# Value products of a 16-head attention, two key blocks at a time behind every second block's scores

## Chip, cores and metric

The kernel runs on 1 core of one Trainium2 chip. The metric is the device time of one execution in microseconds (us). Three timed runs of the kernel before gave 745.59, 741.81 and 741.84 us, median 741.84 us.

## What is computed

Three stages follow each other in one launch: a bucketed softmax attention (2 batches of 8 heads, 768 rows, 64 columns a head), a two-layer network with a squared ReLU over 1536 tokens, and a mixture of 8 experts with one expert a token. The change touches the attention alone:

```python
mask = q_bucket[:, :, :, None] == k_bucket[:, :, None, :]      # sign bits of q @ proj and k @ proj
scores = scale * np.matmul(q, k.transpose(0, 1, 3, 2))
scores = np.where(mask, scores, -1000000000.0)
scores = scores - np.max(scores, axis=-1, keepdims=True)
attn = np.exp(scores)
attn = attn / (np.sum(attn, axis=-1, keepdims=True) + 1e-09)
return np.matmul(attn, v).astype(np.float32)
```

## The kernel before, in words

The 16 heads (2 batches times 8) are numbered h = 0 to 15, two heads make a pair p, and each head has NB = 6 key blocks j of 128 keys. `Attn.program` (L482) writes out the order of the whole attention by hand: `at(g, pri, fn)` puts a step into group g with a priority, the list is sorted by 10 g + pri, and every engine gets its instructions in that order. Group g = 6 h + j holds block j of head h. For the heads from 4 on a group holds, in this order:

- `st(h, j)` (L396, priority 1): the scores of one key block against all 768 queries, four matmuls of 384 columns (tile `Sst`). ScalarE takes the exponential into the tile `e` (L405), and, except for block 5, makes a 16-bit copy `eh` (L411); GpSimd makes the rest `el = e - eh` (L412).
- `maxp` of the head two further on (L350, priority 2, 12 groups ahead): two matmuls (tile `Smaxp`) and a VectorE maximum `mx` (L359).
- `avs(h, j, t)` (L418), the value products of the block two groups back (`LAG = 2`), in two halves t = 0 and 1 at priorities 5 and 7 (`a0`, `a1`): 18 matmuls for a block with `eh` and `el`, and for block 5 (`WHOLE`) 6 matmuls on the 32-bit `e` (tile `VW`) with 6 on the small tiles `NM` and `VS`. They add up in a tile `av` of their own (pool `psA`).

Once a head or once a pair of heads other steps stand in a group, at priority 8 behind both halves or at 0 ahead of the scores: `mrow` (L383, tile `Smrow`, once a head in the group of a block 2), `xt` (L455, tile `Sxt`, ahead of a block 4), the two `trans` (L185, tiles `Strans` of q and of k) and `bits` (L235, tile `Sbits`).

What ties these steps together is the pool `psS` (L1363, opened in `fused_kernel`, 3 buffers): `Sst`, `Smaxp`, `Smrow`, `Sxt`, `Strans` and `Sbits` all come from it, each of two PSUM banks. Three tiles are there, so a step on TensorE that needs a new one waits until the reader of an older one is done: ScalarE's exponential for `Sst`, VectorE's maximum for `Smaxp`.

```python
psA = pool("psA", 1, **P)
psS = pool("psS", 3, cs, **P)
```

Behind the attention, from about group 81 on, the decoding of the next stage's weights (`w_next`, L659, lines L705 to L735) is mixed into the same queues of ScalarE, VectorE and GpSimd; the 16 groups of heads 14 and 15 have no `maxp`.

Of the kernel before, what the change touches and what calls it, by code (L numbers as in the profile page):

```python
# [25 lines left out]
LAG = 2  # L26
# [3 lines left out]
XN = [[f"x{g}{i}" for i in "hl"] for g in range(3)]  # L30
AT = dict(vx=-2, tq=-20, tk=-19, bits=-17, mo=-6, mr=2, xt=21, mx=-12, vs=4,
          tpri=8, bpri=0, vpri=8, mopri=6, mrpri=8, xpri=8, fpri=3, mxpri=2, a0=5, a1=7)


def f(ap):
# [7 lines left out]
class Attn:  # L43
# [438 lines left out]
    def program(self):  # L482

        ev = []

        def at(g, pri, fn, *a):
            ev.append((10 * g + pri, len(ev), fn, a))

        NP = self.NP
        n = iter(range(-100, -9))  # L490
        pre = lambda fn, *a: at(next(n), 0, fn, *a)
        gp = self.nc.gpsimd
        pre(self.load, 0)
        pre(self.setup2)
        pre(self.zero_set, gp, 0)
        pre(self.setup2b)
        for p in range(1, 4):
            pre(self.zero_set, gp, p)
        for p in range(1, 4):
            pre(self.load_v, p)  # L500
        pre(self.trans, 0, "q")
        pre(self.asm, 0, "q", (0,))
        pre(self.trans, 0, "k")
        pre(self.asm, 0, "k", (0,))
        pre(self.bits0, "q")
        pre(self.bits0, "k")
        pre(self.setup3)
        for x in "qk":
            pre(self.asm, 0, x, (1,))
        pre(self.load_v, 0, self.nc.sync)  # L510
        for x in "qk":
            pre(self.asm, 1, x, (0,))
        pre(self.load, 1)
        for x in "qk":
            pre(self.asm, 1, x, (1,))
        pre(self.maxp, 0, 0)
        pre(self.maxp, 0, 1)
        pre(self.bits1, 0)
        pre(self.maxp, 0, 2)
        pre(self.vabs, 0)  # L520
        for j in range(3, NB):
            pre(self.maxp, 0, j)
        pre(self.vscan, 0, 1)
        pre(self.mops, 0)
        pre(self.bits2, 0)
        pre(self.asm_aux, 1)
        pre(self.mrow, 0)
        pre(self.vscale0, 0)
        pre(self.vscale1)
        at(0, 2, self.vscale2, 0)  # L530
        at(0, 2, self.vxs, 0)
        pre(self.vmask)
        at(1, 2, self.vx, 0)
        at(1, 6, self.vsums, 0, 1)
        for hh in range(2):
            at(1 + hh, 4, self.vxl, 0, hh)
        for i, p in enumerate(range(1, 4)):
            at(1 + 2 * i, 9, self.vabs, p)
            at(3 + 2 * i, 9, self.vred, p)
        at(6, 9, self.vscale0, 1)  # L540
        at(8, 0, self.vscale1)
        at(9, 4, self.vscale2, 1)
        at(9, 9, self.vscan, 1, 4)
        at(10, 9, self.vsums, 1, 4)
        for i, p in enumerate(range(4, NP)):
            at(6 + i, 9, self.load_v, p)
            at(13 + 2 * i, 9, self.vabs, p)
            at(14 + 2 * i, 9, self.vred, p)
        at(20, 9, self.vscale0, 2)
        at(22, 0, self.vscale1)  # L550
        at(23, 4, self.vscale2, 2)
        at(23, 9, self.vscan, 4, 8)
        at(24, 9, self.vsums, 4, 8)
        for j in range(NB):
            at((1, 1, 2, 2, 3, 3)[j], 3, self.maxp, 1, j)
            at((6, 7, 7, 8, 8, 9)[j], 3, self.maxp, 2, j)
            at((10, 11, 11, 12, 13, 13)[j], 2, self.maxp, 3, j)
        for p in range(NP):
            g = 12 * p
            if p:  # L560
                if p > 1:
                    at(g - 32 + 3 * (p == 3), 0, self.load, p)
                s = ((0, 1, 4), (7, 8, 9))[p - 1] if p < 3 else (g + AT["tq"], g + AT["tk"], g + AT["bits"])
                for n, x in enumerate("qk"):
                    at(s[n], AT["tpri"], self.trans, p, x)
                    if p == 1:
                        at(2, 6, self.asm, 2, x, (0,))
                        at(2, 7, self.asm, 2, x, (1,))
                        at(4, 9, self.asm, 3, x, (0,))
                        at(5, 4, self.asm, 3, x, (1,))  # L570
                    else:
                        at(s[1] + 1, 6, self.asm, 2 * p, x)
                        at(g - 12, 0, self.asm, 2 * p + 1, x)
                at(s[2], AT["bpri"], self.bits, p)
                at(s[2], 9, self.asm_aux, 2 * p)
                at(5 if p == 1 else g - 12, 0, self.asm_aux, 2 * p + 1)
                at(g - (4 if p > 1 else 3), 9, self.vxs, p)
                at(g - 2, AT["vpri"], self.vx, p)
                for hh in range(2):
                    at(g - 1 + 2 * hh, AT["vpri"], self.vxl, p, hh)  # L580
            at(g + AT["vs"], 9, self.vsel, p)
            if p < NP - 1:
                at(g + AT["xt"], AT["xpri"], self.xt, p)
        for h in range(2 * NP):
            for j in range(NB):
                g = 6 * h + j
                i = g % 12
                at(g, 1, self.st, h, j)
                if h > 3:
                    at(g + AT["mx"], AT["mxpri"], self.maxp, h, j)  # L590
                at(g + LAG, AT["a0"], self.avs, h, j, 0)
                at(g + LAG, AT["a1"], self.avs, h, j, 1)
            g = (-29, 4, 9, 14)[h] if h < 4 else 6 * h + AT["mo"]
            if h:
                at(g, 4 if h < 4 else AT["mopri"], self.mops, h)
                at((0, 5, 10, 16)[h] if h < 4 else g + AT["mr"], (0, 0, 7, 8)[h] if h < 4 else AT["mrpri"], self.mrow, h)
            at(6 * h + 6 + LAG, AT["fpri"], self.fin, h)
        ev.sort(key=lambda e: e[:2])
        return [(e[0] // 10, (lambda e=e: e[2](*e[3]))) for e in ev]
# [876 lines left out]
```

## Time and profile before

| | |
|---|---|
| median of 3 runs | 741.84 us |
| the profiled execution, its own time | 740.73 us |
| span of that execution's profile | 738.9 us |
| TensorE busy, matmuls | 691.1 us (94%) |
| TensorE busy, weight loads | 606.7 us (82%) |
| VectorE / ScalarE / GpSimd busy | 429.1 / 364.6 / 248.0 us |
| mean granted TensorE clock | 0.975 of full speed |

The time is the whole device execution; the span is what the profile of one execution covers, 1.8 us less. PE is TensorE's matmuls, PEld its weight loads, DVE is VectorE, ACT ScalarE, POOL GpSimd. Matmuls overlap in the records, so their busy time reads higher than what is really filled; the weight loads stand behind each other.

### The profile page before, as it was taken

The numbers are of one execution on the slowest core, as the hardware profiler recorded it, in microseconds if no ns is written. First come the engines' busy times: TensorE is split into PE (matmuls) and PEld (weight loads), VectorE is DVE, ScalarE is ACT, GpSimd is POOL, SyncE is SP. The second block draws the span as 40 slices with busy tenths as digits, with TensorE's granted clock in tenths as the row PEclk, the third lists the DMA queues.
The fourth block names the chain that finished last, engine by engine and source line by source line (L and its number), as shares of the span: only waits on it lengthen the run. The fifth ranks groups of instructions, "written<-read, shape, count | busy, mean of one in ns | idle before, by whom it ended". The sixth has DMA issues, their size and how long they took to land.

```text
span 738.9 us, 12831 instructions
## 1 busy us (share of the span) xinstructions
PE 691.1 (94%) x5037; PEld 606.7 (82%) x5037; DVE 429.1 (58%) x781; ACT 364.6 (49%) x562; POOL 248.0 (34%) x251
## 2 busy tenths in 40 slices
PE   6688899999999689999999999999999999999993
PEld 5487789899898568788888888888789889999992
DVE  5456767667667977888783322235663674545311
ACT  2565787877878755555542232222350344344412
POOL 8295877776878860000000000200020104040102
PEclk9799999999999889999999999999999999999997
DMA  6979435655470221443420010001440545445101
GB/s 147 218 168 226 98 73 113 141 110 114 109 186 2 87 86 59 151 134 114 142 59 0 1 44 14 1 16 43 130 144 1 175 157 191 129 136 151 58 17 44
DMA packets 53509, 73.64 MB, mean 100 GB/s; under 512 B 30456, under 2 KB 30968, under 8 KB 53440
## 3 DMA queue, kind: packets, MB, share of 16 engines
q1 hardware_dynamic: 50320, 63.49, 32.6%
q0 software_dynamic: 2960, 9.24, 4.0%
q8 instruction: 41, 0.67, 0.4%
q14 instruction: 28, 0.23, 0.1%
q10 hardware_dynamic: 160, 0.00, 0.0%
HBM read 46.37 MB, written 6.49 MB: 72 GB/s over the span
## 4 chain that ended last, share of the span: by engine, by line
PE 68%; ACT 8%; issue 7%; DVE 7%; POOL 4%; DMA 3%; SPq 1%; POOLq 0%; ACTq 0%; DVEq 0%
PE Y L863 17%; PE H L820 16%; PE H L1161 8%; PE Y L1181 7%; PE Sst L403 5%; PE av L424 5%; ACT e L405 4%; PE Smaxp L357 2%; PE Sbits L240 2%; POOL el L412 2%; ACT eh L411 1%; PE ml L891 1%; DVE v L716 1%; DMA nq<-in_q_dram 1%; PE Strans L192 1%
## 5 line engine op out<-in xcount | busy, mean ns | idle before, releaser
L412 POOL TENSOR_TENSOR el<-e,eh 128x768 f16<-128x768 f32 x80 | 133.3, 1673 | 64.5 <-ACT eh L411 52.6
L863 PE MATMUL Y<-gh,W 128*128 128x512 f32 x384 | 131.8, 396 | 0.7 <-DVE sv L873 0.7
L359 DVE TENSOR_REDUCE mx<-Smaxp 128x1 f32<-128x768 f32 x96 | 90.3, 953 | 37.9 <-PE Smaxp L357 37.6
L405 ACT ACTIVATE e<-Sst 128x768 f32<-128x768 f32 x96 | 77.0, 803 | 44.6 <-PE Sst L403 42.4
L403 PE MATMUL Sst<-Q,K 128*128 128x384 f32 x384 | 93.5, 366 | 2.1 <-ACT e L405 1.9
L863 PEld LDWEIGHTS Y<-gh,W 128*128 128x128 f32 x384 | 72.1, 188 | 16.8 <-DVE sv L873 1.1
L1181 PE MATMUL Y<-hh,W 128*128 128x408 f32 x256 | 81.5, 359 | 0.0
L827 DVE SCALAR_TENSOR_TENSOR r<-r,sb 128x512 f32<-128x512 f32 x46 | 35.9, 780 | 70.3 <-ACT r L826 70.3
L863 PE MATMUL Y<-gl,W 128*128 128x512 f32 x192 | 75.3, 392 | 0.0
L403 PEld LDWEIGHTS Sst<-Q,K 128*128 128x128 f32 x384 | 65.3, 195 | 5.7 <-ACT e L405 2.8
L411 ACT ACTIVATE eh<-e 128x768 f16<-128x768 f32 x80 | 67.5, 844 | 2.5
L826 ACT ACTIVATE r<-H 128x512 f32<-128x512 f32 x44 | 26.3, 598 | 82.0 <-PE H L820 81.9
L801 POOL IOTA ev<- 128x96 f32 x1 | 0.3, 298 | 192.7 <-PE H L820 192.7
L357 PE MATMUL Smaxp<-K,Q 96*128 96x384 f32 x192 | 50.6, 353 | 10.6 <-DMA Q<-aux 3.5
L1134 POOL DMA_INDIRECT xg<-yd,ix x16 | 17.8, 1110 | 123.2 <-DVE nf L1120 62.8
L834 ACT ACTIVATE gh<-r,sb 128x512 fp32r<-128x512 f32 x46 | 33.1, 721 | 52.7 <-PE Y L863 51.0
L835 DVE SCALAR_TENSOR_TENSOR gl<-r,sb,gh 128x512 fp32r<-128x512 f32 x46 | 34.4, 749 | 37.4 <-ACT gh L834 37.4
L424 PE MATMUL av<-VX,eh 128*128 128x65 f16 x960 | 52.1, 196 | 4.1 <-ACT eh L411 4.1
L424 PEld LDWEIGHTS <-eh 128*128 128x128 f16 x960 | 39.8, 99 | 16.7 <-issue 11.5
L1068 DVE TENSOR_TENSOR W<-st,W 128x1024 fp32r<-128x1024 f32 x32 | 38.8, 1224 | 18.4 <-ACT W L1067 18.4
L1181 PEld LDWEIGHTS Y<-hh,W 128*128 128x128 f32 x256 | 48.0, 188 | 0.0
L357 PEld LDWEIGHTS Smaxp<-K,Q 96*128 96x128 f32 x192 | 35.6, 197 | 14.7 <-issue 4.0
(321 smaller groups left out, 1475.1 us busy)
## 6 DMA issues: line engine op xcount, KB each, us to landing
st<-in_moe_w_dram SPq DMA_DIRECT2D x32, 512.0 KB
sw<-in_moe_w_in_dram SPq DMA_DIRECT2D x16, 512.0 KB
sw<-in_moe_w_out_dram SPq DMA_DIRECT2D x16, 512.0 KB
Q<-qh SPq DMA_DIRECT2D x32, 192.0 KB
K<-kh SPq DMA_DIRECT2D x32, 192.0 KB
nq<-in_q_dram SPq DMA_DIRECT2D x16, 192.0 KB
nk<-in_k_dram SPq DMA_DIRECT2D x16, 192.0 KB
Q<-ql SPq DMA_DIRECT2D x16, 192.0 KB
```

The source lines that it names most:

```text
L357: nc.tensor.matmul(out=ps[:, a, 0:HALF], lhsT=self.Q1[i][0:96, j * 128:j * 128 + 128], rhs=self.K1[i][0:96, a * HALF:a * HALF + HALF])
L359: nc.vector.tensor_reduce(out=self.mx[h][:, j:j + 1], in_=ps[:, :, 0:HALF], axis=AX.XY, op=ALU.max)
L403: nc.tensor.matmul(out=ps[:, a, 0:HALF], lhsT=K[:, c], rhs=Q[:, a * HALF:a * HALF + HALF], start=(n == 0), stop=(n == 1))
L405: nc.scalar.activation(out=h2(e), in_=ps[:, :, 0:HALF], func=ACTF.Exp, scale=0.125)
L411: nc.scalar.activation(out=eh, in_=e, func=ACTF.Copy)
L412: nc.gpsimd.tensor_tensor(out=el, in0=e, in1=eh, op=ALU.subtract)
L424: mm = lambda q, n, e, v, start=False, stop=False: nc.tensor.matmul(out=av[:, q, 0:n], lhsT=e, rhs=v, start=start, stop=stop, skip_group_c ...
L820: nc.tensor.matmul(out=ps, lhsT=w[:, k, fs], rhs=x[:, k], start=(n == 0), stop=(n == 11))
L863: nc.tensor.matmul(out=self.yp[d], lhsT=w[:, i, ds], rhs=x, start=(fc in (0, FA) and n == 0), stop=(fc in (FA - 1, 15) and n == 2))
L1068: nc.vector.tensor_tensor(out=lo[:, o], in0=d["st"], in1=f(hi[:, o]), op=ALU.subtract)
L1161: nc.tensor.matmul(out=ps, lhsT=w, rhs=xx[:, kd, 0:C], start=(n == 0), stop=(n == 11))
L1181: nc.tensor.matmul(out=self.yp[d][:, 0:C], lhsT=w, rhs=xx, start=(fc == 0 and n == 0), stop=(fc == 7 and n == 2))
```

## The change

The value products of the even blocks (j = 0, 2, 4) of heads 4 to 13 move one group later. They then stand in the group of the odd block with that block's own value products: first half of the even block, first half of the odd block, second halves likewise. In the group of an even block no value product is left. This makes 30 pairs of blocks, in groups (26, 27) to (84, 85). Nothing is added or removed: the instructions of ScalarE, VectorE, GpSimd and the DMA queue are the same in the same order, and only TensorE's differ in their order.

```diff
+AV2 = (4, 14)
...
-                at(g + LAG, AT["a0"], self.avs, h, j, 0)
-                at(g + LAG, AT["a1"], self.avs, h, j, 1)
+
+                ga = g + LAG + (j % 2 == 0 and AV2[0] <= h < AV2[1])
+                at(ga, AT["a0"], self.avs, h, j, 0)
+                at(ga, AT["a1"], self.avs, h, j, 1)
```

Two places show it on TensorE. The numbers in the names tell tiles apart; a wait named Activation is one for ScalarE, DVE for VectorE, Pool for GpSimd.

The first place is head 8, blocks 2 and 3, with `mrow` between them. Before ("..." leaves out rows of the same step):

```order
L403 MATMUL Sst_2524<-Q1_0_114,K1_0_115 128x384 [waits DVE_49]
...
L357 MATMUL Smaxp_2535<-K1_2_123,Q1_2_122 128x384 [waits Activation_49]
...
L424 LDWEIGHTS eh_2464
L424 MATMUL av0_2543<-VX0_132,eh_2464 128x65
...
L389 MATMUL Smrow_2562<-identb_59,MP1_131 128x128 [waits DVE_49]
L403 MATMUL Sst_2569<-Q1_0_114,K1_0_115 128x384 [waits Activation_49]
```

In the changed kernel:

```order
L407 MATMUL Sst_2524<-Q1_0_114,K1_0_115 128x384 [waits DVE_49]
...
L361 MATMUL Smaxp_2535<-K1_2_123,Q1_2_122 128x384 [waits Activation_49]
...
L393 MATMUL Smrow_2543<-identb_59,MP1_131 128x128 [waits DVE_49]
L407 MATMUL Sst_2550<-Q1_0_114,K1_0_115 128x384 [waits Activation_49]
...
L361 MATMUL Smaxp_2561<-K1_2_123,Q1_2_122 128x384 [waits DVE_49]
...
L428 LDWEIGHTS eh_2464
```

The value products on `eh_2464` stood between the maximum's matmuls and `mrow`; now they come behind the second scores and their maximum. The second scores take the tile that the first scores had, three tiles back, and wait for ScalarE in both orders.

The second place is head 8, blocks 0 and 1, with no step between them; the second block's group also holds the value products of a block 5. Before:

```order
L403 MATMUL Sst_2457<-Q1_0_114,K1_0_115 128x384 [waits DMAHW6_49,DMAHW5_49,DVE_49]
...
L357 MATMUL Smaxp_2469<-K1_2_123,Q1_2_122 128x384 [waits DMAHW3_49,DMAHW4_49,DMAHW0_49,Activation_49]
...
L424 LDWEIGHTS eh_2392
...
L403 MATMUL Sst_2496<-Q1_0_114,K1_0_115 128x384 [waits DVE_49]
...
L357 MATMUL Smaxp_2507<-K1_2_123,Q1_2_122 128x384 [waits Activation_49]
...
L424 MATMUL av1_2313<-VW1_135,e_2424 128x65 x3
```

In the changed kernel, from the second scores on:

```order
L407 MATMUL Sst_2478<-Q1_0_114,K1_0_115 128x384 [waits DVE_49]
...
L361 MATMUL Smaxp_2489<-K1_2_123,Q1_2_122 128x384 [waits Activation_49]
L361 MATMUL Smaxp_2489<-K1_2_123,Q1_2_122 128x384
L428 LDWEIGHTS eh_2392
L428 MATMUL av1_2337<-VX1_133,eh_2392 128x65
```

The value products on `eh_2392` have moved from ahead of the second scores to behind the second maximum. That maximum takes the tile of the first scores, three tiles back, and waits for ScalarE in both orders.

The third place is head 7, blocks 0 and 1, with `bits` between them. Before:

```order
L403 MATMUL Sst_2204<-Q1_3_126,K1_3_127 128x384 [waits DMAHW7_49,DMAHW0_49,DVE_49]
...
L424 LDWEIGHTS eh_2126
...
L240 MATMUL Sbits_2249<-qh_2159,WQ0_110 128x384 [waits Activation_49]
...
L240 MATMUL Sbits_2249<-kl_2201,WK0_112 128x384 [waits DVE_49]
```

In the changed kernel:

```order
L361 MATMUL Smaxp_2216<-K1_1_119,Q1_1_118 128x384
L244 MATMUL Sbits_2231<-qh_2141,WQ0_110 128x384 [waits Activation_49]
...
L361 MATMUL Smaxp_2257<-K1_1_119,Q1_1_118 128x384 [waits DVE_49]
...
L428 LDWEIGHTS eh_2126
```

Here too the value products that stood ahead of `bits` now stand behind the second maximum; `bits` takes the tile of the first scores of this pair and waits for their exponential.

## Rows read from the trace of the kernel before

**Rows 1.** The page, part 1: busy time, share of the span and instructions.
```profile
PE 691.1 (94%) x5037; PEld 606.7 (82%) x5037; DVE 429.1 (58%) x781; ACT 364.6 (49%) x562; POOL 248.0 (34%) x251
```
**Rows 2.** Busy time by stretch: PE, PEld, DVE, ACT, POOL; PEclk, DMA share, GB/s.
```profile
178.00:206.00 28.00, 27.46 (x326) 25.28 (x326) 19.59 (x32) 21.83 (x32) 21.85 (x20) 1.00 0.45 111
...
231.00:263.00 32.00, 25.07 (x303) 21.56 (x301) 28.75 (x31) 23.68 (x37) 25.86 (x19) 0.89 0.16 51
```
**Rows 3.** Timeline, weight loads, head 10 blocks 0 to 4: start, us, instruction, [idle before].
```profile
186.71 0.65 PEld L403 LDWEIGHTS Sst<-Q,K 128*128 128x128 f32 x4
...
187.87 0.24 PEld L424 LDWEIGHTS <-eh 128*128 128x128 f16 x6 [0.15 <-issue]
...
188.40 0.65 PEld L403 LDWEIGHTS Sst<-Q,K 128*128 128x128 f32 x4
189.03 0.36 PEld L357 LDWEIGHTS Smaxp<-K,Q 96*128 96x128 f32 x2
189.38 0.81 PEld L424 LDWEIGHTS av<-VW,e 128*128 128x128 f32 x6
...
191.02 0.65 PEld L403 LDWEIGHTS Sst<-Q,K 128*128 128x128 f32 x4
...
192.95 0.65 PEld L403 LDWEIGHTS Sst<-Q,K 128*128 128x128 f32 x4
...
194.63 0.65 PEld L403 LDWEIGHTS Sst<-Q,K 128*128 128x128 f32 x4
```
**Rows 4.** Timeline, ScalarE, the exponential of head 10 block 2.
```profile
192.09 0.81 ACT L405 ACTIVATE e<-Sst 128x768 f32<-128x768 f32 x1 [0.93 <-PE Sst L403]
```
**Rows 5.** Timeline, weight loads, from k's transpose to head 11 block 2.
```profile
198.96 0.64 PEld L192 LDWEIGHTS Strans<-ident,nk 128*128 128x128 f32 x6 [0.28 <-ACT e L405]
...
201.49 0.65 PEld L240 LDWEIGHTS Sbits<-qh,WQ 128*128 128x128 f32 x4 [0.17 <-ACT e L405]
...
206.19 0.65 PEld L403 LDWEIGHTS Sst<-Q,K 128*128 128x128 f32 x4
```
**Rows 6.** Timeline, ScalarE, the same stretch.
```profile
199.87 0.81 ACT L196 ACTIVATE kh<-Strans 128x768 fp32r<-128x768 f32 x1 [0.96 <-PE Strans L192]
200.62 0.81 ACT L405 ACTIVATE e<-Sst 128x768 f32<-128x768 f32 x1
```
**Rows 7.** Timeline, weight loads, head 9 blocks 2 to 5.
```profile
178.60 0.65 PEld L403 LDWEIGHTS Sst<-Q,K 128*128 128x128 f32 x4
...
182.22 0.64 PEld L471 LDWEIGHTS Sxt<-ident,xn 128*128 128x128 f32 x6
...
185.03 0.65 PEld L403 LDWEIGHTS Sst<-Q,K 128*128 128x128 f32 x4 [0.45 <-ACT e L405]
```
**Rows 8.** Timeline, matmuls, the same stretch.
```profile
182.25 0.85 PE L471 MATMUL Sxt<-ident,xn 128*128 128x128 f32 x6
...
185.03 0.97 PE L403 MATMUL Sst<-Q,K 128*128 128x384 f32 x4 [0.33 <-ACT e L405]
```
**Rows 9.** Timeline, ScalarE, the same stretch.
```profile
182.67 0.84 ACT L411 ACTIVATE eh<-e 128x768 f16<-128x768 f32 x1
183.42 0.58 ACT L477 ACTIVATE x0h<-Sxt 128x512 fp32r<-128x512 f32 x1
...
184.16 0.81 ACT L405 ACTIVATE e<-Sst 128x768 f32<-128x768 f32 x1
```
**Rows 10.** Waits of the stretch 104 to 231 us: in total, times, longest.
```profile
PEld L424 <- issue: 7.1, 46, 0.2
```
**Rows 11.** Groups of instructions of the same stretch: count, busy, mean ns, idle before.
```profile
L412 POOL TENSOR_TENSOR el<-e,eh 128x768 f16<-128x768 f32 x47 | 77.3, 1652 | 29.8 <-ACT eh L411 22.7 <-PE Smaxp L357 2.2 <-POOL el L412 2.0
```
**Rows 12.** The chain that ended last, 225 to 290 us: start, us, what.
```profile
237.33 0.86 DVE mx L359
238.20 1.69 DVE sw L713
...
262.05 0.51 issue
```

## The prediction

> **What bounds the kernel now.** I read the page's busy shares first, then busy time by stretch, then the timeline of weight loads in one period of the attention, and beside it ScalarE's timeline. TensorE is busy 94% of the span [rows 1], and between 104 and 231 us, where heads 4 to 13 run, its clock is full: in 178 to 206 us the granted clock reads 1.00 (the 2.4 GHz level), weight loads fill 25.28 of 28 us, and VectorE, ScalarE and GpSimd are each busy about 20 to 22 of 28 [rows 2]. So TensorE's order sets the pace there, and weight loads stand behind each other almost without holes. The pattern repeats every 12 blocks (one pair of heads), 27.59 us from 178.60 to 206.19 [rows 5, 7].
>
> A plain block is 1.69 us (186.71 to 188.40): 1.16 to the first value product (scores, maximum, and a hole of 0.15 at the switch from the 32-bit to the 16-bit loads), then 0.53 for the value products. A block whose value products are those of a block 5 takes 2.62 us (188.40 to 191.02), 0.98 up to them and 1.64 for them, with no such hole ahead [rows 3]. The hole is counted 46 times in 104 to 231 us, 7.1 us in all [rows 10].
>
> The number that decides is how long a score tile stays occupied. Scores start at 191.02; their exponential runs from 192.09 for 0.81 us; the next user of that tile starts at 192.95: **1.93 us from start to release** [rows 3, 4]. Before the change the 0.53 us of value products and the hole stand inside these 1.93 us. There TensorE loses next to nothing to the wait: that block with its `mrow` would have ended around 192.8 by itself (191.02 + 1.69 and one short load).
>
> **The change, part by part.** Nothing is added; 27 pairs of blocks lie in groups 26 to 79, three more in the stretch where the weights are decoded. The score pool's tiles go round in the same order in both kernels. In a changed pair, scores, maximum, any step between, scores and maximum follow directly, and both blocks' value products come last. What the pool needs for the fourth tile of that run is the tile of the pair's first scores, so 1.93 us must pass, and only the work left in between hides it. The pairs of one period:
>
> - Blocks 0 and 1 of an even head. Now 186.71 to 191.02, 4.31 us [rows 3]. Changed: the second maximum would start at 1.01 + 0.63 = 1.64 us (scores and maximum of a block without the hole are 189.38 less 188.40, 0.98 to 1.01; scores alone are 189.03 less 188.40) but waits to 1.93; then 0.35 for it, the hole 0.15, 0.53 and 1.64: 4.60. Cost 0.29.
> - Blocks 2 and 3, `mrow` between. Now 191.02 to 194.63, 3.61 us [rows 3]. Changed: the second scores wait to 1.93 with only about 1.2 us of work ahead; then 1.16 and twice 0.53: 4.15. Cost 0.54, one whole block of value products that used to stand under the exponential.
> - Blocks 4 and 5 with q's transpose between, then blocks 0 and 1 of the odd head with k's transpose ahead and `bits` between. Now 194.63 to 206.19, 11.56 us. The first of the two would take 1.93 + 1.16 + 1.06 = 4.15, but k's transpose waits for an exponential anyway and starts at 4.33 (198.96) [rows 5], so nothing is lost there. `bits` starts 2.53 us behind that transpose, set by ScalarE's chain (copy of k at 199.87, exponential at 200.62 for 0.81 [rows 6]), and that chain stays. What stood under it, the hole and 0.53, now comes later. Cost 0.68.
> - Blocks 2 and 3 of the odd head with `mrow`, then `xt`, then blocks 4 and 5. Now 178.60 to 186.71, 8.11 us [rows 3, 7]. Changed: the first pair takes 4.15, so `xt` starts at 4.15 instead of 3.62 (182.22). Its result is there 0.88 later (182.25 + 0.85 against 182.22 [rows 8]), at 5.03, while ScalarE takes it up at 4.82 now (183.42), right behind its 16-bit copy [rows 9]. ScalarE therefore slips by 0.21, and the release of block 4's scores from 6.43 (185.03) to 6.64; then 1.16 and twice 0.53: 8.86. Cost 0.75.
>
> One period costs 0.29 + 0.54 + 0.68 + 0.75 = 2.26 us. Groups 26 to 73 are four periods: 9.0. Groups 74 to 79 have no transposes left: 0.54 for the `mrow` pair, 0.11 for a plain pair (1.93 + 0.35 + 0.15 + 1.06 = 3.49 against 3.38) and 0.29: 0.9. The sum is **10.0 us**.
>
> On the gain side stand only the holes. A period has ten now and keeps eight: the `mrow` pairs go back to 16-bit loads and out again between the blocks, so they keep two. This is already in the sums above; alone it is 2 times 0.15 in each of five periods, 1.5 us.
>
> From group 80 on I charge nothing. From 231 to 263 us VectorE is busy 28.75 of 32 us [rows 2] and carries the chain, from the first decode at 238.20 to 262 [rows 12]; weight loads fill only 21.56 of the 32. The cover is VectorE's decoding; without it the last three pairs would cost up to 1.0 more (0.75 and 0.29). The delay built up before is not absorbed: the first decode stands behind a maximum of the attention (237.33) in VectorE's queue [rows 12], so it starts later with TensorE.
>
> What is late next behind the wait: GpSimd's `el`, 1.65 us each, ten a period with other work, 21.85 of 28 us busy [rows 2, 11]. By estimate a pair's last 16-bit copy ends 4.4 us after the pair's start (1.07 and four ScalarE operations of 0.81 to 0.84) and its `el` at 6.1; the products that need it start at 4.15 + 1.93 + 1.16 + 0.53 = 7.8. I take no loss. The queues of the DMAs are not passed by anything.
>
> The sum stands against the profiled execution's 740.73 us: 750.7. The median of the runs is 741.84, so I predict 741.84 + 10.0 = **751.8 us**.
>
> **A rule against the trace.** Two records at 185.03, the matmul that waited and the weight load of the same scores, start together, behind a hole of 0.45 in the loads [rows 7, 8]: the load did not run ahead of the wait. By the Trainium skill, TensorE: Matmul & The Clock Gate, section "Architectural detail: the array is 16× 32×32, not 1× 128×128", TensorE's queue pulls weight loads ahead of matmuls in flight. By that rule a load would be done within the wait; the row speaks against it for these 32-bit scores.
>
> **Rivals.**
>
> - Weight loads run ahead of the wait. A load of the scores is 0.65 / 4 = 0.16 us [rows 3], and 27 waits would each get one back: 4.3 us, so 747.5. The release of 1.93 was read from start to start and would already hold such a gain; chance 0.06.
> - The release takes longer than 1.93. With ScalarE's other copies in the way it is already 2.17 in one pair of six (scores behind the 0.64 of `xt`'s loads from 182.22, release 185.03 [rows 7]). If the bunched maxima and exponentials make it that in 20 more pairs, or `el` comes late by as much, 20 times 0.24 is 4.8: 756.6. Chance 0.12.
> - Not slower: the delay is eaten in 231 to 263 us. TensorE has about 10 us of unfilled weight-load time there [rows 2], as much as the sum. If the decoding began at a time of its own (its data's arrival), TensorE would come 10 us late into a stretch where it waits anyway, and the time would stay at 741.8. It decides if the first decode does not move with the attention; its place right behind a maximum [rows 12] speaks against it. Chance 0.03.
> - Only the holes count: if ScalarE freed a score tile in 1.6 us, no wait would show and 1.5 us are gained: 740.3. The exponential alone ends 1.88 after the start [rows 3, 4]. For more than 0.5% (3.7 us) every pair would have to lose a hole, 30 times 0.15, 737.3. Chance 0.02, and 0.02 for that second form.
>
> That the change does nothing is excluded: TensorE's rows differ in the three places shown.
>
> **How the numbers follow.** The forecast case has 0.75. Its range goes from the least (weight loads partly ahead, some waits covered: 747) to the last three pairs counted and ScalarE late in places (757); with the neighbouring rivals I take 746.5 to 757.5, which leaves out the not-slower cases and the long tail of late releases. Within 0.5% of 741.84 (3.7 us, about what a measurement here can tell from no change) lie the eaten delay and the lone holes: 0.05. Faster by more: 0.02. Slower by more: 0.93.
>
> **What would show it.** Right: weight loads of the second scores behind `mrow`, and of the second maximum elsewhere, idle 0.3 to 0.7 us before them, released by the exponential; a period of about 29.8 us instead of 27.59; 16-bit holes down from ten to eight a period; the first decode near 248 us instead of 238.20; the rest shifted as a block. Wrong: a period under 28.5, or a first decode that has not moved, or idle time that GpSimd's `el` ends.

## The result, and the profile after

The changed kernel takes 748.26 us (median of 9 runs, 747.74 to 750.41) against 741.81 us of the kernel before in the same series (9 runs). The ratio is 1.0103, with a 95% interval of 1.008 to 1.0127: 7.6 us slower (5.9 to 9.4). The ratio is not that of the two medians, which differ by 6.45 us. Forecast were 751.8 us, 10.0 us slower, in a range of 746.5 to 757.5.

The page, part 1, of the changed kernel (its profiled execution took 750.41 us, span 748.6), to be read beside [rows 1]:

```profile
PE 696.3 (93%) x5037; PEld 610.2 (82%) x5037; DVE 427.2 (57%) x781; ACT 364.3 (49%) x562; POOL 248.0 (33%) x251
```

Counts are the same, and so nearly are the busy times of VectorE, ScalarE and GpSimd. TensorE's records are 5.2 us (matmuls) and 3.5 us (weight loads) longer in sum, but hardly where heads 4 to 13 run. There the time came as idle time. To see it, take the same work in both kernels, from the exponential of head 4 block 2 to that of head 13 block 2, called the **stretch** from here on. Its busy times (columns as in [rows 2]) before and after:

```profile
109.28:231.10 121.82, 119.81 (x1427) 110.06 (x1425) 85.85 (x138) 94.96 (x138) 94.47 (x73) 1.00 0.53 117
```

```profile
111.05:241.60 130.55, 120.93 (x1427) 109.64 (x1425) 83.97 (x138) 95.33 (x138) 94.78 (x73) 1.00 0.49 110
```

The clock is full in both. Weight loads fill 109.64 us instead of 110.06 although the stretch is 8.73 us longer, and the other engines are nearly as busy as before: every engine waits more. The waits of the weight loads show for whom TensorE waits (idle time in total, times, longest). Before, in 104 to 231 us and beside the holes of [rows 10], they are:

```profile
PEld Sst L403 <- ACT e L405: 1.8, 4, 0.5
PEld Strans L192 <- ACT e L405: 1.0, 4, 0.3
PEld Sbits L240 <- ACT e L405: 0.7, 4, 0.2
```

After, the same from 105.8 to 241.5 us, where the same blocks now run:

```profile
PEld Sst L407 <- ACT e L409: 9.8, 13, 0.9
PEld L428 <- issue: 4.4, 28, 0.2
PEld Sbits L244 <- ACT e L409: 3.7, 4, 0.9
PEld L393 <- issue: 1.4, 9, 0.2
PEld Smaxp L361 <- ACT e L409: 1.1, 6, 0.2
```

Waits for ScalarE's exponential went from 3.5 us (12) to 14.6 us (23). The holes at the switch of loads went from 46 (7.1 us) to 37 (28 + 9, 5.8 us). GpSimd's `el` ends none of them. Here is one period, the timeline of weight loads from head 9 block 2 to head 11 block 2 of the changed kernel (columns as in [rows 3]):

```profile
185.45 0.65 PEld L407 LDWEIGHTS Sst<-Q,K 128*128 128x128 f32 x4
...
187.38 0.65 PEld L407 LDWEIGHTS Sst<-Q,K 128*128 128x128 f32 x4 [0.68 <-ACT e L409]
...
189.64 0.64 PEld L475 LDWEIGHTS Sxt<-ident,xn 128*128 128x128 f32 x6
190.25 0.65 PEld L407 LDWEIGHTS Sst<-Q,K 128*128 128x128 f32 x4
...
192.18 0.65 PEld L407 LDWEIGHTS Sst<-Q,K 128*128 128x128 f32 x4 [0.94 <-ACT e L409]
...
194.40 0.65 PEld L407 LDWEIGHTS Sst<-Q,K 128*128 128x128 f32 x4
...
196.29 0.30 PEld L361 LDWEIGHTS Smaxp<-K,Q 96*128 96x128 f32 x2 [0.16 <-ACT e L409]
...
198.86 0.64 PEld L407 LDWEIGHTS Sst<-Q,K 128*128 128x128 f32 x4
...
200.80 0.65 PEld L407 LDWEIGHTS Sst<-Q,K 128*128 128x128 f32 x4 [0.67 <-ACT e L409]
...
203.03 0.65 PEld L407 LDWEIGHTS Sst<-Q,K 128*128 128x128 f32 x4
...
204.90 0.65 PEld L407 LDWEIGHTS Sst<-Q,K 128*128 128x128 f32 x4
...
207.18 0.64 PEld L196 LDWEIGHTS Strans<-ident,nk 128*128 128x128 f32 x6
...
209.71 0.65 PEld L244 LDWEIGHTS Sbits<-qh,WQ 128*128 128x128 f32 x4 [0.93 <-ACT e L409]
...
215.07 0.65 PEld L407 LDWEIGHTS Sst<-Q,K 128*128 128x128 f32 x4
```

The `mrow` pair at 185.45 waits 0.68 us at its second scores, which start 1.93 us behind the first ones. The same wait stands at 200.80, behind `mrow`, 1.94 us after 198.86. From 185.45 to 215.07 a period lasts 29.62 us; it was 27.59.

The stretch serves below as the yardstick for all kernels. It was 121.82 us (109.28 to 231.10) and is 130.55 us (111.05 to 241.60): 8.73 us more. It is used because head 4 block 2, which comes ahead of every changed instruction, stands anywhere from 107.22 to 113.99 us in the executions profiled here; the spans carry that difference, the stretch does not. Behind the stretch the chain of waits of the changed kernel reads:

```profile
248.68 1.68 DVE sw L719
...
272.81 0.51 issue
...
279.57 3.44 PE SH L826 x12
```

Against [rows 12] the first decode is at 248.68 instead of 238.20 and the end of decoding at 272.81 instead of 262.05: 10.48 and 10.76 later, of which 8.73 is the stretch and 1.77 the later start of this execution. The decoding absorbed nothing of the delay.

### The profile page after: what moved, and what is told of

Its sections match the earlier page's. It is cut to its first block, busy times and chain, and to the rows that moved or that the text cites. A ratio compares the mean times of both kernels' runs of the same rounds, so it can differ in the third digit from the quotient of the medians.

```text
span 748.6 us, 12831 instructions
## 1 busy us (share of the span) xinstructions
PE 696.3 (93%) x5037; PEld 610.2 (82%) x5037; DVE 427.2 (57%) x781; ACT 364.3 (49%) x562; POOL 248.0 (33%) x251
## 4 chain that ended last, share of the span: by engine, by line
PE 69%; DVE 7%; issue 6%; ACT 6%; POOL 4%; DMA 4%; SPq 2%; POOLq 0%; ACTq 0%; DVEq 0%
PE Y L869 16%; PE H L826 16%; PE av L428 7%; PE Sst L407 7%; PE H L1167 6%; PE Y L1187 5%; PE Smaxp L361 3%; ACT e L409 3%; PE Sbits L244 2%; PE Strans L196 1%; POOL el L416 1%; PE ml L897 1%; DVE v L722 1%; SPq L187 1%; SPq L210 1%
## 5 line engine op out<-in xcount | busy, mean ns | idle before, releaser
L407 PE MATMUL Sst<-Q,K 128*128 128x384 f32 x384 | 95.2, 372 | 8.7 <-ACT e L409 8.5
L407 PEld LDWEIGHTS Sst<-Q,K 128*128 128x128 f32 x384 | 67.4, 200 | 13.6 <-ACT e L409 11.7
```

Source lines behind the costliest of these rows:

```text
L407: nc.tensor.matmul(out=ps[:, a, 0:HALF], lhsT=K[:, c], rhs=Q[:, a * HALF:a * HALF + HALF], start=(n == 0), stop=(n == 1))
```

## Experiments

Each edit is against the changed kernel. Ratios are to the kernel before, on the same chip.

**1. `mrow` behind the pair.** In the changed kernel only `mrow`'s load of 0.10 us stands between the first maximum and the second scores, which take the first scores' tile. With `mrow` out of the middle the pair is a plain one, in which the second maximum takes that tile.

```diff
-at(... g + AT["mr"], ..., self.mrow, h)
+at(... g + AT["mr"] + (5 <= h <= 14), ..., self.mrow, h)
```

> The changed kernel with mrow of heads 5 to 14 moved one group later, behind both blocks' value products. Yardstick: from the exponential of head 4 block 2 to that of head 13 block 2, 121.8 us before and 130.55 changed; 12 blocks are 27.59 and 29.62. Theory A (a score tile is released 1.9 us after its scores start, and only the work between hides that): the mrow pairs no longer need that tile for the second scores but for the second maximum, later by 0.65; a pair of 4.17 becomes about 3.6. Period about 28.8, stretch about 126.7, time about 4 us under the changed kernel's. Theory B (two blocks' work handed to ScalarE and GpSimd at once comes back late, wherever the other steps stand): period stays near 29.6, stretch near 130.5. Theory C (the wait is due to mrow's own operands): the wait moves with mrow, idle time ahead of its load, period near 29.6.

Stretch 128.17, period 29.11 (expected: 126.7 and 28.8), and 749.08 us (4 runs), ratio 1.0123 (1.0075 to 1.017). The `mrow` pairs became 3.51 and 3.46 us (195.20 to 198.71, 211.06 to 214.52) from 4.17 and 4.19, but part came back later, in new waits for `mrow`'s reader (`NM`). Timeline of weight loads, from head 10 block 3 on:

```profile
197.14 0.30 PEld L361 LDWEIGHTS Smaxp<-K,Q 96*128 96x128 f32 x2 [0.23 <-ACT e L409]
...
198.68 0.10 PEld L393 LDWEIGHTS <-MP 128*128 128x128 bf16 x1
...
200.17 0.64 PEld L196 LDWEIGHTS Strans<-ident,nq 128*128 128x128 f32 x6 [0.45 <-ACT NM L396]
...
216.95 0.30 PEld L361 LDWEIGHTS Smaxp<-K,Q 96*128 96x128 f32 x2 [1.06 <-ACT NM L396]
...
217.64 0.65 PEld L407 LDWEIGHTS Sst<-Q,K 128*128 128x128 f32 x4 [0.39 <-ACT e L409]
```

`mrow` too takes a score tile. It is now read late in ScalarE's queue, behind exponentials, so its tile comes free late. Ahead of `mrow`'s own load (198.68) stands no wait, so its operands were not the cause. The stretch gives back 2.4 of 8.7 us; the timed ratio, of four runs, is not below that of the changed kernel and does not show it.

**2. `bits` behind the value products.** `bits` of the pairs of heads from 4 on moves from between the two scores to behind both blocks' value products.

```diff
-at(s[2], AT["bpri"], self.bits, p)
+at(s[2], 8 if p > 3 else AT["bpri"], self.bits, p)
```

> The changed kernel with bits of pairs 4 to 7 of heads moved from between the two blocks to behind both blocks' value products. Theory A: bits no longer stands under ScalarE's chain (copy of k, then exponential); the 0.93 us of idle time ahead of it goes, of which about 0.3 comes back ahead of the second maximum. 0.6 a period: period about 29.0, stretch about 128.0, time about 2.5 us under the changed kernel's. Theory B: period stays near 29.6.

Stretch 130.46, ratio 1.0123 (1.0071 to 1.0174): the expected 128.0 was missed. The wait did not go; it changed its bearer, as the timeline of weight loads at head 11 blocks 0 and 1 shows:

```profile
207.18 0.65 PEld L407 LDWEIGHTS Sst<-Q,K 128*128 128x128 f32 x4
...
209.11 0.65 PEld L407 LDWEIGHTS Sst<-Q,K 128*128 128x128 f32 x4 [0.93 <-ACT e L409]
...
212.37 0.65 PEld L244 LDWEIGHTS Sbits<-qh,WQ 128*128 128x128 f32 x4
```

The second scores now take the tile that `bits` took, and wait the same 0.93 us, 1.93 us behind the first scores. The wait belongs to the tile, not to the step that takes it. My expectation had overlooked that.

**3. Only the second halves moved.** The first half (0.27 us of value products and a hole) stays between the two scores, half of the cover.

```diff
-at(ga, AT["a0"], self.avs, h, j, 0)
+at(g + LAG, AT["a0"], self.avs, h, j, 0)
```

> The changed kernel with the first half of the even blocks' value products left in their own group, so that only the second half (0.27 of 0.53 us) moves. Theory A: a half left in place covers 0.27 of the release and the hole 0.15; the mrow pair, bits and the xt pair each cost 0.27 instead of 0.54 to 0.75, the plain pairs nothing. 0.8 a period: period about 28.4, stretch about 125.3, time about 3.5 us over the kernel before. Theory B: half the work bunched, half the cost, stretch about 126.2; near, so this run is a dose, not a verdict. If the cost were the switch between 32-bit and 16-bit loads alone, the switches are those of the kernel before and the stretch would be 121.8.

Stretch 124.84, period 28.3, 744.75 us (10 runs), ratio 1.0053 (1.0027 to 1.0079). Timeline of weight loads, the `mrow` pair of head 10 and then `bits`:

```profile
197.76 0.65 PEld L407 LDWEIGHTS Sst<-Q,K 128*128 128x128 f32 x4
...
199.69 0.65 PEld L407 LDWEIGHTS Sst<-Q,K 128*128 128x128 f32 x4 [0.42 <-ACT e L409]
...
208.34 0.64 PEld L244 LDWEIGHTS Sbits<-qh,WQ 128*128 128x128 f32 x4 [0.44 <-ACT e L409]
```

The wait behind `mrow` is 0.42 with half of the value products left in place and 0.68 with none: 0.26 for half a block. The distance from first to second scores is 1.93 in both, and 1.93 in the kernel before, where the whole block fitted inside [rows 3]. At `bits`, whose wait was 0.17 [rows 5], it is 0.44 and 0.93. This is the dose test of the theory, and the stretch came out 0.5 under its number of 125.3. The kernel has the holes of the kernel before (46, 7.2 us in the same blocks) and is still 3.0 us longer in the stretch, so the switches between the loads are not the cost.

**4. The other pairing.** Blocks (1, 2), (3, 4), (5, 0 of the next head) share their value products; as many pairs, as much bunching, but other steps stand between. The step that reads a head's finished value products off `av` (`fin`) moves behind them.

```diff
-ga = g + LAG + (j % 2 == 0 and AV2[0] <= h < AV2[1])
+ga = g + LAG + (j % 2 == 1 and AV2[0] <= h < AV2[1])
...
-at(6 * h + 6 + LAG, AT["fpri"], self.fin, h)
+at(6 * h + 6 + LAG, 9 if AV2[0] <= h < AV2[1] else AT["fpri"], self.fin, h)
```

> The same bunching with the other parity: the value products of the odd blocks of heads 4 to 13 wait for the next even block, and fin of these heads stands behind them. mrow, q's transpose and bits now fall behind the bunched products without being moved; k's transpose and xt stand between the two scores. Theory A: only those two (of six pairs) need the first scores' tile early, and the waits that the kernel before has ahead of k's transpose (0.28) and bits (0.17) go. Summing a period: 4.55 + 4.1 + 4.15 + 2.0 + 4.55 + 4.15 + 3.5 = 27.0 to 27.6; stretch 119 to 122, time between 2.5 us under the kernel before and the same. Theory B: bunched as in the changed kernel, so as slow: period near 29.6, time 6 to 8 us over the kernel before.

Stretch 123.70, periods 27.62, 28.24, 28.22 and 28.32, 744.28 us (12 runs), ratio 1.0044 (1.0018 to 1.007). The stretch is 1.7 us over the first theory's 119 to 122 and far from the second's, which would be about that of the changed kernel. The time, 3.3 us over the kernel before (1.3 to 5.2), lies between the two and does not decide. The longest waits of this kernel's weight loads, 104 to 232.9 us (idle in total, times, longest):

```profile
PEld Smaxp L361 <- ACT e L409: 3.6, 14, 0.3
PEld Strans L196 <- ACT e L409: 3.5, 4, 0.9
PEld L428 <- issue: 3.2, 20, 0.2
PEld Sst L407 <- DVE aux L252: 2.8, 4, 0.7
...
```

Holes fell from 46 to 20, and yet the kernel is slower than before. Plain pairs now wait 0.24 to 0.33 us at the second maximum. The pair with both transposes waits 0.9 us a period, and one wait I had not foreseen is VectorE reading the tile of `bits` (`aux`), which had been covered. Bunching itself is not the cost: the same number of pairs costs 1.9 us of the stretch instead of 8.7 where other steps stand between the scores.

**5. Two pairs a period that looked free**, (2, 3)'s products behind q's transpose and a block 5 with the next block 0.

```diff
-ga = g + LAG + (j % 2 == 0 and AV2[0] <= h < AV2[1])
+ga = g + LAG + (AV2[0] <= h < AV2[1] and (j == 5 if h % 2 else j == 2))
...
-at(6 * h + 6 + LAG, AT["fpri"], self.fin, h)
+at(6 * h + 6 + LAG, 9 if h % 2 and AV2[0] <= h < AV2[1] else AT["fpri"], self.fin, h)
```

> Bunched only where the release theory sees no loss: the value products of a block 5 of an odd head wait for the next head's block 0 (then mrow follows them), and those of block 2 of an even head wait for block 3, in the pair that has q's transpose between. By the traces of the changed kernel and of the one with odd blocks waiting: the first saves about 0.11 a period (4.44 against 4.55), the second 0.18 (4.15 against 4.33, k's transpose no longer waits). Theory A: period about 27.3, stretch about 120.5, time 1 us or so under the kernel before, too little for the time to show alone. Any theory in which bunching costs by itself: two of six pairs bunched, a third of the changed kernel's 8.7, stretch about 124.7.

Stretch 121.94 against 121.82; 740.27 us (12 runs), ratio 1.0011 (0.999 to 1.0032): no difference. The pair at q's transpose takes 4.32 us in both kernels (111.83 to 116.15 before, 115.29 to 119.61 here). The second scores there start 2.04 us behind the first. Timeline of weight loads:

```profile
117.33 0.64 PEld L407 LDWEIGHTS Sst<-Q,K 128*128 128x128 f32 x4 [0.29 <-ACT e L409]
...
217.94 0.64 PEld L407 LDWEIGHTS Sst<-Q,K 128*128 128x128 f32 x4 [0.68 <-DVE mx L363]
```

The nine holes saved (46 to 37, 7.1 to 5.8 us) went into waits for score tiles. The two middle periods of the stretch are 27.44 and 27.41 us, against 27.59 and 27.63 before, so some 0.2 us of the hoped 0.3 a period was there (at the first one the new order moves the mark itself). The wait at 217.94, which stands once and has no counterpart in the kernel before, took it back; its reason was not followed up. Neither number came out for the stretch: the gain of 1.3 us is not there, and the cost of bunching (124.7) is not there either. No version beat the kernel before.

**6. The last three pairs alone, and all but these.** The prediction charged nothing from group 80 on. Four runs ask whether that holds.

```diff
-AV2 = (4, 14)
+AV2 = (13, 14)
```

> The kernel before with only head 13's even blocks moved: the three pairs in groups 80 to 85, where the weights' decoding on VectorE carries the chain. The prediction charged nothing for them, with up to 1.0 us if the decoding were no cover. Cover theory: stretch head 4 block 2 to head 13 block 2 as before (121.8), first decode 7.1 us behind the exponential of head 13 block 2 as before (231.10 to 238.20), time as before. Otherwise: first decode 0.5 to 1.0 later, time up to 1.0 us over the kernel before.

742.9 us (10 runs), ratio 1.0042 (1.0016 to 1.0068), stretch 121.77. To see what is spread and what is cost, the same kernel again, beside one in which no head is changed (`AV2 = (4, 4)`), and one with heads 4 to 12 changed (`AV2 = (4, 13)`):

> No head is changed (the range of heads is empty), so every engine has the order of the kernel before. Theory (only moved value products cost): the time of the kernel before, ratio 0.998 to 1.002, stretch 121.8. Rival (the small excess of the run with the last three pairs comes from the spread between chips and executions at the start of the program, not from the moved products): this kernel too can read up to 1.004 while its stretch stays at 121.8, with head 4 block 2 at 111 us or later instead of 109.

> The same kernel as the run with the last three pairs alone, beside a kernel without any moved product on the same chip. If the moved products behind group 80 cost something (about 0.4%, 3 us), it reads 2 to 4 us more than the kernel without moved products. If the prediction's step (nothing from group 80 on) holds, the two agree within 1.5 us, and the first decode stands 7.1 us behind the exponential of head 13 block 2 again.

> Heads 4 to 12 changed, head 13 (the last three pairs, groups 80 to 85) not. Stretch 130.5 as in the changed kernel in both theories. If the last three pairs cost nothing, the time is that of the changed kernel, ratio 1.009 to 1.012. If they cost 3 us, ratio 1.005 to 1.007.

| heads changed | us (runs) | ratio to before | stretch | first decode to end of the fourth |
|---|---|---|---|---|
| none | 739.70 (12) | 0.9991 (0.9962 to 1.0021) | 121.85 | 22.77 |
| 13 | 742.90 (10) | 1.0042 (1.0016 to 1.0068) | 121.77 | 24.17 |
| 13, again | 741.30 (12) | 1.0012 (0.9985 to 1.0039) | 121.84 | 24.18 |
| 4 to 12 | 748.57 (7) | 1.0104 (1.0065 to 1.0143) | 130.46 | 22.73 |
| 4 to 13 | 748.26 (9) | 1.0103 (1.008 to 1.0127) | 130.55 | 24.15 |

In time the last three pairs cost 3.1 us once, and 1.6 us against the unchanged order on the same chip, with intervals that overlap; taking them out of the changed kernel gains nothing that can be seen. The first decode starts 7.0 us behind the exponential of head 13 block 2 in all five and in the kernel before: up to there the three pairs cost nothing. Behind it the profiles differ: VectorE's four decodes take 24.15 to 24.18 us in the three executions of this table with head 13 paired, and 22.73 and 22.77 in the two without. Of the other executions, experiments 1 and 2 move the even blocks of head 13 too and show 24.4 and 24.1, and experiment 4 shows 22.8. The kernel before itself, whose order is that of the first line, shows 23.89 (238.12 to 262.01; the chain in [rows 12] counts the first decode from the end of the maximum, 238.20). The difference has a place: small VectorE operations ahead of the second decode and its first operation, `sw`. In the changed kernel VectorE's timeline has:

```profile
255.49 1.55 DVE L376 TENSOR_TENSOR MP<-mc,MP 128x6 bf16<-128x6 f32 x1
```

GpSimd's timeline of the same kernel has beside it:

```profile
255.38 1.64 POOL L416 TENSOR_TENSOR el<-e,eh 128x768 f16<-128x768 f32 x1
```

With no head changed, VectorE's timeline has:

```profile
245.00 0.17 DVE L376 TENSOR_TENSOR MP<-mc,MP 128x6 bf16<-128x6 f32 x1
245.08 0.42 DVE L719 TENSOR_SCALAR sw<-sw 128x512 int32<-128x512 int32 x1
```

And GpSimd's, with no head changed:

```profile
245.06 1.94 POOL L416 TENSOR_TENSOR el<-e,eh 128x768 f16<-128x768 f32 x1
```

Where GpSimd's `el` begins first, at 255.38, the VectorE operation of 6 columns ends with it (257.04 and 257.02). Where VectorE is 0.06 us ahead, it takes 0.17 us. By the Trainium skill, SBUF — State Buffer, section "SBUF: two separate sides", VectorE and GpSimd share a pair of ports that one of them holds for a whole instruction while the other is blocked, also for a VectorE operation with two inputs in SBUF against a GpSimd operation that reads SBUF. The rows at 255.38 and 255.49 agree.

In the kernel before, the 6-column operation took 0.17 us too (244.60), but the next one did not come through; `el` had begun at 244.66. VectorE's timeline of the kernel before:

```profile
244.69 1.92 DVE L713 TENSOR_SCALAR sw<-sw 128x512 int32<-128x512 int32 x1
```

So 1.1 of the 1.4 us between 22.77 and 24.15 can come and go without any change of order. What the pairing adds is a delay: the `el` before that one starts 10.94 us behind the exponential of head 13 block 2 in the changed kernel and 10.37 with no head changed, because the scores ahead of it now stand behind the value products of two blocks (8.18 instead of 7.63 us).

## Why the prediction was right, and where its sizes were off

The sign, the mechanism and the range held: a score tile was released 1.87 to 1.94 us behind the start of its scores in the period shown, against the 1.93 assumed, and value products that had hidden this were moved out of it. The time came 2.4 us below the forecast by the ratio, 1.3 of which the stretch shows in its terms:

- **Blocks 0 and 1 of an even head.** Predicted 4.60, measured 4.46 (194.40 to 198.86). The second maximum started 1.89 us behind the first scores instead of 1.93, and the record of its two loads is 0.30 instead of 0.35. That is no load gone ahead of the wait: each single load keeps its 0.19 us (196.29 and 196.40), they only start 0.11 us apart instead of the 0.18 of the two at 189.03 in the kernel before. The scores' loads kept their full 0.65 behind a wait, and started 1.93 or 1.94 after the first scores. So the rival "weight loads run ahead" falls at both.
- **Blocks 2 and 3 with `mrow`.** Predicted 4.15, measured 4.17 and 4.19.
- **Both transposes.** The step "k's transpose waits for an exponential anyway and starts at 4.33" failed by 0.18: it started at 4.15 (203.03 to 207.18) with no wait. The scores ahead of it start 1.87 behind their pair's first (204.90), not 2.30 as in the kernel before (194.63 to 196.93), so their exponential comes earlier as well, and what the transpose waited for was ready (it ended at 207.12). From there to the next pair 7.89 us against 7.91, with `bits` 2.53 behind the transpose exactly as assumed.
- **`mrow` pair, `xt` and blocks 4 and 5.** Predicted 8.86, measured 8.95 (4.19 and 4.76).
- **The period** grew by 2.03 instead of 2.26; four of them by 8.08 instead of 9.0 (118.48 against 110.40). What follows up to head 13 block 2 grew by 0.65 instead of 0.9.
- **Nothing from group 80 on.** In time this cannot be told from the data. The mechanism that had been priced at up to 1.0 us (second scores that wait) cost nothing, since the first decode kept its distance of 7.0 us. In VectorE's rows behind it the step is off by 0.3 us against the kernel before and by 1.4 us against the run with no head changed, by the order in which `el` and VectorE's operations meet.
- **The first decode** moved with the attention, so the rival in which the delay is eaten falls. About 0.9 us came back at the first `SH` matmuls, 3.44 us instead of 4.36. This is not put down to the change, since they took 3.39 with no head changed and 3.20 to 4.36 us over the eleven executions profiled.
- **The holes.** Nine of 46 went, 1.3 us, as against 1.5 predicted. They were inside the sums and never worth the waits.

The rival "the release takes longer" falls by the changed kernel itself: 1.93 and 1.94 us behind `mrow`, 1.87 in the pair with q's transpose, 1.93 at `bits` and 1.93 behind `xt` (190.25 to 192.18), the one pair in which the kernel before had some 2.2. Experiments 2 and 3 show 1.93 again. Longer ones do occur under other edits, each time with another copy ahead of the exponential in ScalarE's queue: 2.04 in experiment 5, 2.20 in experiment 4 (186.94 to 189.14) and 2.40 in experiment 1 (215.24 to 217.64). That bunching costs by itself is refuted by experiments 4 and 5. Two things stay open: what the last three pairs cost in time (3.1 and 0.9 us over the kernel before by the two ratios, the second not clear of nothing), and why the stretch's 8.73 us read 7.6 in the ratio, which the interval allows.

## What to carry to other kernels

Before work is grouped to save switches, ask what it stands under: with a few rotating tiles, the work between a tile's use and its next one is the cover of the read in between, and the time from use to release, read from the trace from start to start, says how much is needed. A switch saved was worth 0.15 us at most here, a wait uncovered 0.2 to 0.9 us. Moving the step that waits does not help where the next taker of the same tile inherits the wait (experiment 2), and a step moved late holds its own tile longer (experiment 1).

## What the runs showed of the hardware that was not expected

A VectorE operation of 0.17 us can take 1.2 to 1.55 us behind a GpSimd operation that started 0.1 us earlier, so a shift of 0.2 us between two engines' orders moves the end of a 24 us chain by 1.4 us (24.15 and 22.77 us). The same order gave 23.89 and 22.77 us in two executions.

The same twelve `SH` matmuls took 4.36 us in the kernel before and 3.39 us with no head changed, the same order. The granted clock differs. Busy time by stretch (columns as in [rows 2]), the kernel before:

```profile
268.80:273.20 4.40, 4.40 (x14) 3.45 (x14) 2.64 (x4) 0.99 (x3) 3.33 (x2) 0.62 0.31 93
```

The same matmuls with no head changed:

```profile
268.10:271.50 3.40, 3.40 (x14) 2.71 (x14) 2.62 (x4) 0.97 (x3) 3.32 (x2) 0.83 0.13 32
```

The clock reads 0.62 and 0.83 over the same work, between the levels of 1.2 and 2.4 GHz: part of it ran at the lower one. The clock accounts for the difference: 4.40 us at 0.62 and 3.40 us at 0.83 are 2.73 and 2.82 us at full speed. In the 6 us from 262 to 268 ahead of it, TensorE had been busy 2.53 us in the one and 2.85 us in the other. A difference of 1 us at such a place is no evidence for or against an edit.
